# An mLSTM layer and a top-1 mixture of experts in one kernel: at most two of GpSimd's indirect DMAs under way, and a planner that knows more waits

## The chip, the cores and the metric

The kernel runs on one core of a Trainium2 chip. The metric is the device time of one execution in microseconds. The core's engines work side by side, each through its own instructions in order: TensorE (PE in the profile), VectorE (DVE), ScalarE (ACT), GpSimd (POOL), and SyncE (SP), which here only issues DMAs and reads two registers. A step on one engine that needs another's result waits for a semaphore.

## The reference

```python
# attention part: q, k, v, o_gate are (4, 8, 768, 40); i_gate, f_gate (4, 8, 768)
for t in range(S):
    m_new = np.maximum(f_gate[:, :, t] + m, i_gate[:, :, t])
    f_stab = np.exp(f_gate[:, :, t] + m - m_new)
    i_stab = np.exp(i_gate[:, :, t] - m_new)
    C = f_stab * C + i_stab * outer(v_t, k_t)        # one 40 x 40 state for each batch and head
    n = f_stab * n + i_stab * k_t
    denom = np.maximum(np.abs(n @ q_t), 1.0)
    y[:, :, t] = sigmoid(o_gate_t) * (C @ q_t) / denom
# the experts: x is y as 3072 rows of 320; 8 experts with 1024 hidden units
logits = x @ w_gate + modality_bias[modality_id]
e_idx = np.argmax(logits, axis=1)
gate_w = softmax(logits)[row, e_idx]
for e in range(8):
    h = np.maximum(x[e_idx == e] @ w1[e], 0.0)
    out[e_idx == e] = gate_w * (h @ w2[e])
```

## The kernel before

`still_arm` is the part that runs for inputs like these; a general part stands behind a branch and runs only if the first one finds that its assumptions don't hold (the word `bword`, computed by `checks`, `check_light`, `check_sums` and `verdict`).

*The work.* The 3072 tokens are cut in 24 chunks of 128. For each chunk, `light` (L1945) or, for the first 64 tokens of each batch, `special` (L2043, L2058) computes the rows of y. `token_rows` gates and divides two chunks at a time: DVE multiplies by the gate (L1961), POOL multiplies by the reciprocal denominators (L1976), and ACT and DVE split each row into a high and a low float16 part (`rows`, L1979, L1624, L1982). `scatter_rows` (L1997) then writes each chunk's rows by an indirect DMA of POOL to `x_s` in DRAM, sorted by modality, since the two modalities go nearly always to one expert each (classes A and B).

*The experts.* The sorted rows are taken in 15 tiles (`STREAM`): A and B in turn, four tiles of 128 rows first, then ten of 256, and a last one of 96. The tiles numbered 0 to 2 get their rows straight from SBUF by products with selection matrices (`select`, L2112, L2120, copied by ACT into `xt`, L2123, L2124). Later tiles get them by a transposing DMA from `x_s` (`load_tile`, L2096), with the token numbers (`load_ids`, L2102); these wait for the scatters of the chunks that the tile needs. `logits` (L2151 and DVE steps) computes each row's gate. `expert` runs the products with w1 into `H` (L2197), ACT's `hh` (L2202) and DVE's `hl` (L2204), which are the high and the low part of the hidden values, the products with w2 into `O` (L2214), ACT's scaling into `ob` (L2221, three buffers), and an indirect DMA of POOL to the output rows (L2222). All products with weights run three times or so, on high and low halves; `load_w` loads the weights of A and then of B in eight pieces each (L1902, through seven `stage` buffers) and splits them (ACT L1903, DVE L1904). Before that SP reads each expert's number from `e_i` (L1858).

*The odd row.* `odd_row` computes the one row that may have gone to a third expert. When all tiles have their gates, DVE sums what marks it (`fpr`, `fs5`), PE spreads it over partitions (L2246), POOL gathers the row into `xrow` by an indirect DMA (L2256), SP loads that expert's whole w1 and w2 (L2264, L2266), DVE does the products (L2269 to L2277), PE sums over partitions (L2280), ACT scales (L2282), and POOL scatters (L2283).

*The order.* Every step is added to a `Plan` with its engine, a duration from a formula, and the names it reads and writes. `Plan.run` computes how late each step may start (`late`, counted back from the end), subtracts `early`, and then simulates: on each engine, in order of time, the ready step with the smallest `late + bias` goes next. `bias` includes `NUDGE`, a number for single steps by their index. `lk=True` says that a step of DVE or POOL can't run beside such a step of the other; the simulation then holds it back. `lat` is added to a step's end. The instructions are emitted in the simulated order, and each engine runs them in that order. `SOON` (20.0) is the `early` of the chunks from 14 on and of most of the odd row; `HOLD` (200) keeps a step from being started earlier than its `late` plus 200. `idle_products` puts products on zeros where the plan sees PE idle between 4 and 60 us (L1731).

Of the kernel before, what the change touches and what calls it, by code (L numbers as in the profile page):

```python
# [16 lines left out]
ALU = mybir.AluOpType  # L17
# [20 lines left out]
class Plan:  # L38
# [6 lines left out]
    DMA_KB = 380.0  # L45
    AHEAD = 200.0
# [33 lines left out]
    def run(self):  # L80
# [29 lines left out]
        dma_free = 0.0  # L110
        port = {"DVE": 0.0, "POOL": 0.0}
        order, start, end = [], [0.0] * n, [0.0] * n
        while len(order) < n:
            best = None
            for name, e in engines.items():
                if not e["wait"] and not e["ready"]:
                    continue
                s = e["free"]
                if not e["ready"]:
                    s = max(s, e["wait"][0][0])  # L120
                if best is None or s < best[0]:
                    best = s, name
            s, name = best
            e = engines[name]
            while e["wait"] and e["wait"][0][0] <= s + 1e-9:
                i = heapq.heappop(e["wait"])[1]
                heapq.heappush(e["ready"], (late[i] + ts[i]["bias"], i))
            i = heapq.heappop(e["ready"])[1]
            t = ts[i]
            if t["lk"]:  # L130
                s = max(s, port["POOL" if name == "DVE" else "DVE"] - self.HOP)
            start[i] = s
            fin = s + t["dur"]
            if t["lk"]:
                port[name] = fin
            e["free"] = fin
            if t["kb"] is not None:
                dma_free = max(dma_free, fin) + t["kb"] / self.DMA_KB
                fin = dma_free + self.DMA_FIRST
            fin += t["lat"]  # L140
            end[i] = fin
            order.append(i)
            for j in succ[i]:
                hop = 0.0 if ts[j]["eng"] == t["eng"] and t["kb"] is None else self.HOP
                ready_at[j] = max(ready_at[j], fin + hop)
# [1404 lines left out]
SOON = 20.0  # L1550
HINT = 12.0
RING = 12
# [41 lines left out]
def still_arm(tc, a, out):  # L1594
# [113 lines left out]
    def load_kv(pr):  # L1708
        dma(373, lambda: sy.dma_start(kvs[pr], a["kvs"][pr]), w=[f"kv{pr}"], bias=FIRST.get("k", 0) if pr == 0 else 0)
# [4 lines left out]
    def load_o(i):  # L1714
        dma(328, lambda: sy.dma_start(og[i % 4], a["ogl"][:, 2 * i:2 * i + 2]), w=[f"og{i % 4}"], bias=FIRST.get(f"o{i}", 0))
# [8 lines left out]
    plan.add("ACT", 1.4, lambda: s_.preload_act_table_set("exp_and_others"), (), ["table"], bias=-90)  # L1724
# [132 lines left out]
    dve(2, lambda: v.tensor_scalar(ss[:, 0:4:3], n1.broadcast_to([P, 2]), float(CAP), None, ALU.is_ge), r=["cum"], w=["ss"])  # L1857
    dve(2, lambda: v.scalar_tensor_tensor(e_i, kd, ss[:, 0:1], km4[:, 2:4], ALU.mult, ALU.add), r=["kd", "km4", "ss"], w=["e_i"])  # L1858
    dve(1, lambda: v.tensor_scalar(ssc, n1, float(CAP), float(CAP), ALU.is_ge, ALU.mult), r=["cum"], w=["ssc"])
# [4 lines left out]
    dve(2, lambda: v.tensor_scalar(ss[:, 1:3], n1.broadcast_to([P, 2]), float(CAP), None, ALU.is_lt), r=["cum"], w=["ss"])  # L1864
# [85 lines left out]
    def token_rows(i):  # L1950
# [37 lines left out]
        for c in (2 * i, 2 * i + 1):  # L1988
            scatter_rows(c)
        dve(640, lambda: v.tensor_reduce(sums[:, 2 * i:2 * i + 2], rows[:, cs, 0:DM], axis=AX.X, op=ALU.add, apply_absolute_value=True),  # L1990
            r=[f"rowh{c0}", f"rowh{c0 + 1}"], w=["sums"], bias=15, nb=45 if i < 4 else None)

    def scatter_rows(c):
        s = c % RING

        def scatter():
# [5 lines left out]
            disjoint("xs", ins)  # L2002
# [234 lines left out]
    def odd_row():  # L2237
# [3 lines left out]
        for i, (t, ks) in enumerate(((u25, ["cst"]), (kmall, [f"km{k}" for k in range(n_)]), (facs, [f"fac{k}" for k in range(n_)]),  # L2241
                                     (ids, [f"ids{k}" for k in range(n_)]))):
            dve(25, lambda i=i, t=t: v.tensor_tensor(fpr[:, 1 + i], fm, t, ALU.mult), r=fms + ks, w=["fpr"])
# [14 lines left out]
            bounds_check=2 * CAP + P - 1, oob_is_err=False), NC), r=["fp_i"] + [f"xs{c}" for c in range(NC)], w=["xrow"])  # L2258
# [9 lines left out]
        plan.early = 0.0  # L2268
# [7 lines left out]
        for f in range(1, NFC):  # L2276
            dve(320, lambda f=f: v.scalar_tensor_tensor(facc, fw2[:, f], fh[:, f:f + 1], facc, ALU.mult, ALU.add), r=["og0", "fh"], w=["facc"], lk=True)  # L2277
        plan.early = SOON
# [10 lines left out]
    def checks():  # L2289
        dve(24, lambda: v.tensor_tensor(okc, cum, lo_f, ALU.is_ge), r=["cum", "cst"], w=["okc"])  # L2290
        dve(24, lambda: v.tensor_tensor(ra, cum, hi_f, ALU.is_le), r=["cum", "cst"], w=["ra"])
# [101 lines left out]
    for k in range(ntile):  # L2393
        while issued < ntile and issued <= k + PRE:
# [16 lines left out]
    def emit(some):  # L2411
        with tc.manual_schedule():
            for i in some:
# [3 lines left out]
                plan.tasks[i]["fn"]()  # L2417

    cut = sum(plan.start[i] < HINT for i in order)
# [147 lines left out]
```

## Time and profile before

| | |
|---|---|
| median of 3 runs | 223.29 us (223.13, 223.29, 226.51) |
| the profiled execution | 222.62 us |
| its span, first to last instruction | 220.9 us |
| PE, DVE, ACT, POOL busy | 206.7, 142.1, 97.0, 86.1 us |
| mean granted TensorE clock | 0.992 |
| DMA | 31.50 MB, mean 143 GB/s |
| POOL's indirect DMAs | 24 of rows, 25 of outputs, 2 of the odd row |

The profile is of one execution. A row of a timeline has the start and the length in us, the engine, the line, the operation, out<-in, and in brackets the idle time of the engine before it and what ended it. "q" behind an engine's name is its queue of instructions that do no arithmetic. In the chain of work that ended last, each piece is what the next one waited for, or the instruction before it on the same engine; "issue" is time in which nothing was waited for that the profile shows.

### The profile page before, as it was taken

The page shows a single profiled execution, that of the slowest core. Times are in us where ns is not written, and L with a number is a line of the kernel's source. Part 1 is how long each engine was busy: PE and PEld are TensorE (multiplying, and loading weights), DVE is VectorE, ACT ScalarE, POOL GpSimd, SP SyncE. Part 2 cuts the span into 40 slices and gives each one's busy share as a digit, 9 for nine tenths or more (in the row PEclk, how much of TensorE's full clock was granted, in tenths as well). Part 3 has the DMA queues.
Part 4 walks back from the last instruction along what each step waited for, and adds up shares of the span by engine and source line. Part 5 has one row for each costly group of instructions (what it writes and reads, how often), then busy time and mean ns, then how long its engine had stood idle before and what let it go on. Part 6 is the DMA issues. An engine that isn't in the chain of part 4 may idle for free.

```text
span 220.9 us, 5482 instructions
## 1 busy us (share of the span) xinstructions
PE 206.7 (94%) x2139; PEld 167.2 (76%) x2139; DVE 142.1 (64%) x421; ACT 97.0 (44%) x200; POOL 86.1 (39%) x98
## 2 busy tenths in 40 slices
PE   7987699999999999999999999999999999998960
PEld 2875589888887877878878768878878787785840
DVE  4789799998679463566386438425324858629960
ACT  2567688684255553342754313314553223143210
POOL 6458569421106716345048723526030120410321
PEclk9999999999999999999999999999999999999996
DMA  6989997989400659202774493202840010493100
GB/s 181 362 273 362 382 381 132 324 144 265 129 0 34 169 164 222 100 3 91 157 133 132 127 224 79 60 34 91 124 87 32 0 59 3 128 309 132 61 0 13
DMA packets 29783, 31.50 MB, mean 143 GB/s; under 512 B 21862, under 2 KB 22408, under 8 KB 29496
## 3 DMA queue, kind: packets, MB, share of 16 engines
q1 hardware_dynamic: 27176, 22.89, 38.9%
q0 software_dynamic: 2432, 8.13, 10.3%
q8 instruction: 18, 0.29, 0.6%
q14 instruction: 13, 0.11, 0.2%
q10 hardware_dynamic: 144, 0.07, 0.1%
HBM read 19.17 MB, written 8.43 MB: 125 GB/s over the span
## 4 chain that ended last, share of the span: by engine, by line
PE 68%; issue 14%; DMA 5%; POOL 2%; SPq 2%; DVE 2%; ACT 2%; another core or an unknown queue 1%; POOLq 1%; DVEq 0%
PE H L2197 32%; PE O L2214 28%; PE Y L1945 3%; DMA stage<-in_w1p 3%; DMA og<-in_ogl 3%; POOL out L2222 2%; PE M L2151 2%; SPq L1902 1%; PE Y L2043 1%; PE Y L2058 1%; POOLq L2407 1%; DVE hl L2204 1%; PE Y L1810 1%; PE O L2120 0%
## 5 line engine op out<-in xcount | busy, mean ns | idle before, releaser
L2204 DVE SCALAR_TENSOR_TENSOR hl<-H,hh 128x512 f16<-128x512 f32 (+1 forms) x50 | 33.9, 682 | 30.2 <-ACT hh L2202 25.6
L2214 PEld LDWEIGHTS <-hh 128*128 128x128 f16 (+1 forms) x400 | 38.6, 99 | 13.9 <-issue 0.5
L2202 ACT ACTIVATE hh<-H 128x512 f16<-128x512 f32 (+1 forms) x50 | 29.4, 592 | 42.1 <-PE H L2197 37.7
L2222 POOL DMA_INDIRECT out<-ob,ois x25 | 26.1, 1042 | 52.4 <-ACT ob L2221 35.9
L2197 PE MATMUL H<-xt,w1hB 128*128 128x256 f16 (+2 forms) x320 | 45.8, 251 | 0.1
L2197 PE MATMUL H<-xt,w1hA 128*128 128x256 f16 (+1 forms) x280 | 43.5, 257 | 0.3 <-issue 0.3
L2197 PE MATMUL H<-xt,w1lB 128*128 128x256 f16 (+2 forms) x192 | 40.6, 251 | 0.0
L2197 PE MATMUL H<-xt,w1lA 128*128 128x256 f16 (+1 forms) x168 | 37.9, 257 | 1.5 <-DVE w1lA L1904 1.5
L1976 POOL TENSOR_TENSOR xr<-xr,ab 128x640 f32<-128x640 f32 x12 | 17.1, 1424 | 38.9 <-DVE ab L1974 17.3
L2197 PEld LDWEIGHTS <-w1hB 128*128 128x128 f16 x320 | 28.5, 98 | 2.8
L1997 POOL DMA_INDIRECT x_s<-rows,pos_i x24 | 25.3, 1052 | 12.9 <-issue 7.0
L2214 PE MATMUL O<-w2hB,hh 128*128 128x320 f16 (+1 forms) x104 | 28.8, 299 | 0.0
L2214 PE MATMUL O<-w2lB,hh 128*128 128x320 f16 (+1 forms) x104 | 28.7, 299 | 0.0
L2197 PEld LDWEIGHTS <-w1hA 128*128 128x128 f16 x280 | 25.3, 98 | 3.3 <-issue 0.8
L2214 PE MATMUL O<-w2hA,hh 128*128 128x320 f16 x96 | 26.5, 299 | 0.0
L2214 PE MATMUL O<-w2lA,hh 128*128 128x320 f16 x96 | 26.5, 299 | 0.0
L2221 ACT ACTIVATE ob<-O,facs 128x320 f32<-128x320 f32 (+1 forms) x25 | 13.1, 526 | 30.6 <-PE O L2214 20.1
L2214 PEld LDWEIGHTS <-hl 128*128 128x128 f16 (+1 forms) x200 | 19.2, 99 | 8.7 <-DVE hl L2204 1.8
L2197 PEld LDWEIGHTS <-w1lB 128*128 128x128 f16 x192 | 18.7, 98 | 1.6 <-issue 0.3
L2197 PEld LDWEIGHTS <-w1lA 128*128 128x128 f16 x168 | 16.4, 98 | 3.1 <-DVE w1lA L1904 1.7
L2214 PE MATMUL O<-w2hB,hl 128*128 128x320 f16 (+1 forms) x104 | 17.1, 299 | 0.7 <-DVE hl L2204 0.7
L2214 PE MATMUL O<-w2hA,hl 128*128 128x320 f16 x96 | 15.3, 299 | 0.2 <-DVE hl L2204 0.2
(198 smaller groups left out, 294.0 us busy)
## 6 DMA issues: line engine op xcount, KB each, us to landing
qg<-in_ql SPq DMA_DIRECT2D x11, 384.0 KB
og<-in_ogl SPq DMA_DIRECT2D x12, 320.0 KB
stage<-in_w1p SPq DMA_DIRECT2D x8, 384.0 KB
stage<-in_w SPq DMA_DIRECT2D x8, 320.0 KB
stage<-in_w1t SPq DMA_DIRECT2D x1, 1280.0 KB
og<-in_w SPq DMA_DIRECT2D x1, 1280.0 KB
kvs<-in_kvs SPq DMA_DIRECT2D x2, 364.5 KB
sp<-in_spq SPq DMA_DIRECT2D x4, 160.0 KB
```

Of the source, the lines that this page charges most:

```text
L1810: t_.matmul(u3[0:120, g], lhsT=kw[pr][rs, 3 * g:3 * g + 3].rearrange("p h d -> p (h d)"), rhs=kvs[pr][rs, 9 * D + HQ * g:9 * D + HQ * (g + ...
L1902: dma(n // 2, lambda sv=sv, src=src: sy.dma_start(sv, src()), r=[f"reg{c}"], w=[f"stage{k}"])
L1945: t_.matmul(y[p0:p1, HQ * g:HQ * g + w], lhsT=q[0:k, j, g, p0:p1], rhs=s[0:k, g, 0:w], start=(g == 0 and e == 0), stop=(g == 2 and e == n ...
L1976: lane((320 if lane is dve else 290) * n, lambda z=z, f=f, n=n: f(x4[:, z].rearrange("p c h d -> p (c h) d"), x4[:, z].rearrange("p c h d ...
L1997: ins = g_.indirect_dma_start(out=x_s[:, :], out_offset=bass.IndirectOffsetOnAxis(ap=pos_i[:, c:c + 1].bitcast(U32), axis=0), in_=rows[:, ...
L2151: t_.matmul(M0[:, 16 * h:16 * h + 16], lhsT=x[:, b], rhs=wgr[:, b % 3].rearrange("p a e -> p (a e)"), start=(h == 0 and b == 0), stop=(h = ...
L2197: t_.matmul(hp3[:, i], lhsT=l, rhs=r, start=(i == 0 and q == 0), stop=(i == g - 1 and q == 7), skip_group_check=True)
L2202: act(g * n, lambda fl=fl, hp3=hp3: s_.activation(hh[:, fl, 0:n], hp3, AF.Relu), r=[nb], w=[f"hh{j}{f}" for f in range(f0, f0 + g)])
L2204: dve(g * n, lambda fl=fl, hp3=hp3: v.scalar_tensor_tensor(hl[:, fl, 0:n], hp3, 0.0, hh[:, fl, 0:n], ALU.max, ALU.subtract), r=[nb] + [f"h ...
L2214: t_.matmul(op[0:z, 0:DM], lhsT=t[:, f, P * h:P * h + z], rhs=w[:, f], start=(i == 0), stop=(i == 23))
L2221: act(400, lambda h=h, op=op, o=o: s_.mul(obs[o][0:z], op[0:z, 0:DM], facs[0:z, s["q0"] + h:s["q0"] + h + 1]), r=[no, f"fac{k}"], w=[f"ob{ ...
L2222: swdma(164, lambda h=h, o=o: disjoint("outf", g_.indirect_dma_start(out=out[:, :], out_offset=bass.IndirectOffsetOnAxis(ap=ois[0:z, s["q0 ...
```

## The change

1. **At most two under way.** When the instructions are emitted, each indirect DMA of POOL gets a dependency on the one two before it: it is issued when that one has landed. The planner does the same in its simulation (`OUT`, `sent`).
2. **What the planner knows.** DVE's steps with immediates or two operands from SBUF get `lk=True` (`ss`, `e_i`, `ssc`, parts of `odd_row` and `checks`); a step of POOL that may not run beside one of DVE starts 0.17 us behind its end (`LEAD`), not 0.13 ahead of it; four steps get a latency `lat` (the first `kvs`, the first two `og`, the gather of the odd row, its last sum).
3. **The odd row sooner.** Its steps get `early` 30 (`ODD`), where most had 20 and the products 0. `SOON` is 30 for 20.
4. **No explicit table load.** ACT's `preload_act_table_set` (L1724) goes; all later steps' indices fall by one.
5. **Priorities anew.** `NUDGE` has other numbers for many steps. `sums` of the later chunks may not start before 110 us in the plan.

```diff
 NUDGE = {
-    5: -33, 34: 162, 35: 57, 36: 44, 38: 34, 43: -8, 45: -116, 52: -7, ...
+    5: -33, 33: 453, 34: 199, 35: 44, 37: 34, 42: -8, 44: -116, 51: 21, ...
...
+    LEAD = 0.17
+    OUT = 2
...
             if t["lk"]:
-                s = max(s, port["POOL" if name == "DVE" else "DVE"] - self.HOP)
+                s = max(s, port["POOL"] - self.HOP if name == "DVE" else port["DVE"] + self.LEAD)
+            far = name == "POOL" and t["kb"] is not None
+            if far and len(sent) >= self.OUT:
+                s = max(s, sent[-self.OUT])
...
                 fin = dma_free + self.DMA_FIRST
+                if far:
+                    sent.append(fin)
...
-SOON = 20.0
+SOON = 30.0
+ODD = 30.0
...
-    plan.add("ACT", 1.4, lambda: s_.preload_act_table_set("exp_and_others"), (), ["table"], bias=-90)
...
-    dve(2, lambda: v.tensor_scalar(ss[:, 1:3], n1.broadcast_to([P, 2]), float(CAP), None, ALU.is_lt), r=["cum"], w=["ss"])
+    dve(2, lambda: v.tensor_scalar(ss[:, 1:3], n1.broadcast_to([P, 2]), float(CAP), None, ALU.is_lt), r=["cum"], w=["ss"], lk=True)
...
-            r=[f"rowh{c0}", f"rowh{c0 + 1}"], w=["sums"], bias=15, nb=45 if i < 4 else None)
+            r=[f"rowh{c0}", f"rowh{c0 + 1}"], w=["sums"], bias=15, nb=45 if i < 4 else 110)
...
-            bounds_check=2 * CAP + P - 1, oob_is_err=False), NC), r=["fp_i"] + [f"xs{c}" for c in range(NC)], w=["xrow"])
+            bounds_check=2 * CAP + P - 1, oob_is_err=False), NC), r=["fp_i"] + [f"xs{c}" for c in range(NC)], w=["xrow"], lat=3.0)
...
-        plan.early = 0.0
...
-        plan.early = SOON
...
             if issued == ntile:
                 check_sums()
+                plan.early = ODD
                 odd_row()
                 plan.early = SOON
...
-                plan.tasks[i]["fn"]()
-
+                ins = plan.tasks[i]["fn"]()
+                if plan.tasks[i]["eng"] == "POOL" and plan.tasks[i]["kb"] is not None:
+                    if len(sent) >= plan.OUT:
+                        tc.add_manual_dep(ins.ins, sent[-plan.OUT].ins.name,
+                                          mybir.DependencyInfo(mybir.DependencyClass.Sync, mybir.DependencyReason.DATA),
+                                          reason="GpSimd's DMAs under way")
+                    sent.append(ins)
+
+    sent = []
```

More of the change, by code (lines that the diff above doesn't have):

```diff
@@ L1702, in disjoint @@
         tc.add_to_no_dep_group(group, ins.ins)
+        return ins
     dma(64, lambda: s_.dma_start(gq, a["gsq"]), w=["gq"], eng="ACT", bias=-99)
@@ L1708, in load_kv @@
     def load_kv(pr):
-        dma(373, lambda: sy.dma_start(kvs[pr], a["kvs"][pr]), w=[f"kv{pr}"], bias=FIRST.get("k", 0) if pr == 0 else 0)
+        dma(373, lambda: sy.dma_start(kvs[pr], a["kvs"][pr]), w=[f"kv{pr}"], lat=0.5 if pr == 0 else 0.0, bias=FIRST.get("k", 0) if pr == 0 else 0)
     def load_q(i):
@@ L1714, in load_o @@
     def load_o(i):
-        dma(328, lambda: sy.dma_start(og[i % 4], a["ogl"][:, 2 * i:2 * i + 2]), w=[f"og{i % 4}"], bias=FIRST.get(f"o{i}", 0))
+        dma(328, lambda: sy.dma_start(og[i % 4], a["ogl"][:, 2 * i:2 * i + 2]), w=[f"og{i % 4}"], lat=0.9 if i < 2 else 0.0, bias=FIRST.get(f"o{i}", 0))
     load_kv(0)
@@ L1856, in still_arm @@
     ss, ssc = small([4], "ss"), small([1], "ssc")
-    dve(2, lambda: v.tensor_scalar(ss[:, 0:4:3], n1.broadcast_to([P, 2]), float(CAP), None, ALU.is_ge), r=["cum"], w=["ss"])
-    dve(2, lambda: v.scalar_tensor_tensor(e_i, kd, ss[:, 0:1], km4[:, 2:4], ALU.mult, ALU.add), r=["kd", "km4", "ss"], w=["e_i"])
-    dve(1, lambda: v.tensor_scalar(ssc, n1, float(CAP), float(CAP), ALU.is_ge, ALU.mult), r=["cum"], w=["ssc"])
+    dve(2, lambda: v.tensor_scalar(ss[:, 0:4:3], n1.broadcast_to([P, 2]), float(CAP), None, ALU.is_ge), r=["cum"], w=["ss"], lk=True)
+    dve(2, lambda: v.scalar_tensor_tensor(e_i, kd, ss[:, 0:1], km4[:, 2:4], ALU.mult, ALU.add), r=["kd", "km4", "ss"], w=["e_i"], lk=True)
+    dve(1, lambda: v.tensor_scalar(ssc, n1, float(CAP), float(CAP), ALU.is_ge, ALU.mult), r=["cum"], w=["ssc"], lk=True)
     dve(24, lambda: v.scalar_tensor_tensor(ra, C0[:, 32:32 + NC], ssc, cumx[:, 0:NC], ALU.add, ALU.add), r=["cum", "cum0", "H2", "ssc"], w=["ra"])
@@ L2001, in scatter @@
             tc.declare_no_dep(ins.ins, group="reads", reason="rows of tiles that need this chunk are loaded later, others are not in it")
-            disjoint("xs", ins)
+            return disjoint("xs", ins)
         swdma(168, scatter, r=[f"rowh{s}", f"rowl{s}", f"id{s}", "rowz", "pos_i"] + (["prefill0", "prefill1"] if c > 10 else []), w=[f"xs{c}"])
@@ L2079, in behind @@
                               reason="the chunk's rows")
+        return ins
     def no_late(ins, need):
@@ L2242, in odd_row @@
                                      (ids, [f"ids{k}" for k in range(n_)]))):
[L2243 removed]
+            dve(25, lambda i=i, t=t: v.tensor_tensor(fpr[:, 1 + i], fm, t, ALU.mult), r=fms + ks, w=["fpr"], lk=True)
         dve(125, lambda: v.tensor_reduce(fs5, fpr, axis=AX.X, op=ALU.add), r=["fpr"], w=["fs5"])
@@ L2276, in odd_row @@
         for f in range(1, NFC):
-            dve(320, lambda f=f: v.scalar_tensor_tensor(facc, fw2[:, f], fh[:, f:f + 1], facc, ALU.mult, ALU.add), r=["og0", "fh"], w=["facc"], lk=True)
-        plan.early = SOON
+            dve(320, lambda f=f: v.scalar_tensor_tensor(facc, fw2[:, f], fh[:, f:f + 1], facc, ALU.mult, ALU.add), r=["og0", "fh"], w=["facc"], lk=True, lat=2.5 if f == NFC - 1 else 0.0)
         n2, y2 = take("Y")
@@ L2289, in checks @@
     def checks():
-        dve(24, lambda: v.tensor_tensor(okc, cum, lo_f, ALU.is_ge), r=["cum", "cst"], w=["okc"])
-        dve(24, lambda: v.tensor_tensor(ra, cum, hi_f, ALU.is_le), r=["cum", "cst"], w=["ra"])
+        dve(24, lambda: v.tensor_tensor(okc, cum, lo_f, ALU.is_ge), r=["cum", "cst"], w=["okc"], lk=True)
+        dve(24, lambda: v.tensor_tensor(ra, cum, hi_f, ALU.is_le), r=["cum", "cst"], w=["ra"], lk=True)
         dve(24, lambda: v.tensor_tensor(okc, okc, ra, ALU.mult), r=["ra"], w=["okc"], lk=True)
@@ L2416, in emit @@
                     zeros(to, w, to is not M0)
-                plan.tasks[i]["fn"]()
+                ins = plan.tasks[i]["fn"]()
[5 more added lines that the diff above has]
+                    sent.append(ins)
+    sent = []
     cut = sum(plan.start[i] < HINT for i in order)
```

28 rows, old and new, of the table NUDGE are left out of this document.

## The prediction

> **What bounds the kernel now.** I read the page's busy shares first, then busy time by stage, then who TensorE (PE) waited for, then the chain and the timelines of the stages where PE was idle.
>
> ```profile
> span 220.9 us, 5482 instructions
> PE 206.7 (94%) x2139; PEld 167.2 (76%) x2139; DVE 142.1 (64%) x421; ACT 97.0 (44%) x200; POOL 86.1 (39%) x98
> PEclk9999999999999999999999999999999999999996
> ```
>
> PE is busy 94% of the span at the full granted clock, and no other engine reaches 65%. So only PE's 14.2 us without work, and what it does without need, can be won. The stages (columns: stretch, length, busy us and instructions of PE, its weight loads, DVE, ACT, POOL; clock, DMA share, GB/s):
>
> ```profile
> 4.00:16.00 12.00, 11.01 (x106) 8.67 (x105) 8.85 (x37) 6.87 (x20) 6.13 (x12) 1.00 0.93 306
> 16.00:27.40 11.40, 8.05 (x95) 6.45 (x92) 10.02 (x21) 7.77 (x16) 7.94 (x7) 1.00 1.03 373
> 27.40:54.50 27.10, 27.10 (x360) 23.44 (x360) 25.50 (x60) 19.48 (x36) 12.72 (x12) 1.00 0.88 246
> 54.50:120.00 65.50, 65.43 (x650) 53.65 (x648) 41.78 (x115) 30.84 (x68) 27.96 (x25) 1.00 0.45 114
> 120.00:130.00 10.00, 9.47 (x85) 7.20 (x84) 4.10 (x16) 3.05 (x6) 5.83 (x6) 1.00 0.60 158
> 130.00:180.00 50.00, 50.00 (x545) 40.68 (x544) 24.24 (x70) 17.43 (x37) 15.85 (x16) 1.00 0.30 70
> 180.00:200.00 20.00, 19.98 (x177) 16.52 (x174) 12.47 (x47) 7.24 (x13) 3.06 (x3) 1.00 0.47 155
> 200.00:214.30 14.30, 12.91 (x134) 9.52 (x132) 13.00 (x45) 2.53 (x6) 2.96 (x3) 1.00 0.10 39
> 214.30:220.90 6.60, 0.00 (x0) 0.00 (x0) 0.16 (x1) 0.52 (x1) 0.94 (x1) 0.73 0.05 11
> ```
>
> Between 27.4 and 214.3 us PE is idle for 0 + 0.07 + 0.53 + 0 + 0.02 + 1.39 = 2.01 us. The 184.9 us of products there are untouched by the change. What is left to win is those 2.0 us and the start: from 16.0 to 27.4 PE idles 3.35 us, with the DMA engines full (1.03 of their time, 373 GB/s). The last 6.6 us hold the last scatter and the landing of its rows; nothing in the diff shortens them. The waits by name (us in all, times, longest):
>
> ```profile
> PE O L2120 <- ACT xt L2123: 1.8, 1, 1.8
> PE H L2197 <- DVE w1lA L1904: 1.5, 1, 1.5
> PE O L2214 <- DVE hl L2204: 0.9, 2, 0.7
> PE Y L2280 <- DVE facc L2277: 0.7, 1, 0.7
> ```
>
> The first two are the start, the next two the end (the odd row and the DVE steps round it).
>
> **The change, part by part.**
>
> *Steps with immediates marked `lk`.* The 1.5 us wait has its cause in the timelines of DVE and POOL:
>
> ```profile
> 17.57 1.67 DVE L1864 TENSOR_SCALAR ss<-cumx 128x2 f32<-128x2 f32 x1
> 17.93 1.28 POOL L1976 TENSOR_TENSOR xr<-xr,ab 128x640 f32<-128x640 f32 x1
> 19.80 0.95 DVE L1904 SCALAR_TENSOR_TENSOR w1lA<-stage,w1hA 128x768 f16<-128x768 f32 x1
> 20.80 0.23 PE L2197 MATMUL H<-xt,w1lA 128*128 128x128 f16 x1 [1.53 <-DVE w1lA L1904]
> ```
>
> A step on two numbers took 1.67 us, because it overlapped POOL's 1.28 us multiplication: it ended 0.03 us after it. The low weights (L1904) behind it, and PE's first products, came that much later. The planner did not know this kind of step waits; now it does, and can put L1864 elsewhere. That removes the 1.53 us wait, but only a part is gained: the last pieces of the first expert's weights come with full DMA queues anyway, as the chain of this stage shows:
>
> ```profile
> 15.45 5.91 DMA stage<-in_w1p
> 21.38 0.84 ACT w1hA L1903
> 22.23 2.16 another core or an unknown queue
> 24.57 0.60 ACT xt L2123
> 25.22 1.01 PE O L2120 x15
> ```
>
> A piece of weights issued at 15.45 lands 5.91 us later. ACT then stands 2.16 us for something the profile can't name, and PE's 1.8 us wait is its consequence. The new order doesn't remove a cause that I can name here. For the start as a whole, nothing and all of its named waits (1.53 + 1.82 = 3.35 us) are the bounds; I take **-1.5 us**, the first wait, since its cause is the one the planner now sees.
>
> *At most two indirect DMAs under way.* The trace of before has no such wait, so its cost is bounded from the rows of POOL and of SP's queue:
>
> ```profile
> 16.66 1.24 POOL L1997 DMA_INDIRECT x_s<-rows,pos_i  x1 [1.74 <-ACT w2hA L1903]
> 19.37 1.01 POOL L1997 DMA_INDIRECT x_s<-rows,pos_i  x1 [0.16 <-issue]
> 25.04 0.97 POOL L1997 DMA_INDIRECT x_s<-rows,pos_i  x1 [0.30 <-issue]
> 37.65 1.00 POOL L1997 DMA_INDIRECT x_s<-rows,pos_i  x1 [0.17 <-issue]
> 40.23 1.44 POOL L1997 DMA_INDIRECT x_s<-rows,pos_i  x1 [0.30 <-issue]
> 31.04 1.33 SPq L2096 DMA_TRANSPOSE xt<-x_s  x1
> 44.53 2.80 SPq L2096 DMA_TRANSPOSE xt<-x_s  x2
> 54.53 1.75 PE H L2197 x16
> ```
>
> The transposes wait for the scatters (1.0 and 1.8 us of SP's queue in these two places), so the last scatter before each landed no later than its start: 25.04 to 31.04 is 6.0 us, 40.23 to 44.53 is 4.3 us. Six scatters stand from 16.66 to 25.04. With two under way, the third waits for the first, and so on: at 4.3 us each they issue at 16.66, 19.37, 20.96, 23.67, 25.26, 27.97, the last 2.9 us later; at 6.0 us each, at 22.66, 25.37, 28.66, 31.37, the last 6.3 us later. In the next batch of four, the one at 40.23 waits for that of 37.65 to land (41.95): 1.7 us. Behind the waiting scatters stand POOL's multiplications of rows, then those rows' own scatters, then SP's transposes, then the fifth tile's products at 54.53. If that order stays, the transposes come 4.6 to 8.0 us later. They have 10.0 us, of which 1.4 go to the first of the two transposes and 4.3 (an estimate, the scatters' own landing) to its flight: 4.3 us of slack, 2.8 if PE is there 1.5 us earlier. So the price is 0 to 5.2 us. I take **0**: the planner now counts these waits when it picks its order, so it can run multiplications ahead of a blocked scatter. Less than nothing would need the loads to be faster for it; no row shows that. Later batches, of two to five scatters, lie in stages with the DMA engines at 0.30 to 0.60 of their time, where PE has tiles ready; I cost them at 0, and if that cover is gone they cost what the fifth tile's do. The waits themselves sit on POOL, which is 39% busy.
>
> *The odd row sooner.* The tail end of PE, by the timeline:
>
> ```profile
> 190.14 1.05 POOL L2256 DMA_INDIRECT xrow<-x_s,fp_i  x1 [10.24 <-issue]
> 198.24 0.23 DVE L2269 TENSOR_TENSOR xf<-xrow 128x64 f32<-128x64 f16 x1 [2.85 <-DMA xrow<-x_s,fp_i]
> 203.05 0.45 PE L2214 MATMUL O<-w2hB,hl 128*128 128x320 f16 x2 [0.66 <-DVE hl L2204]
> 211.81 0.70 PE L2280 MATMUL Y<-facc,ones_f 128*2 128x320 f32 x2 [0.70 <-DVE facc L2277]
> 215.16 0.94 POOL L2222 DMA_INDIRECT out<-ob,ois  x1 [0.99 <-ACT ob L2221]
> ```
>
> DVE stood 2.85 us for the gathered row, which landed 8.1 us after its issue; that pushed `hl` and cost PE 0.66 us, and the row's sum came 0.70 us after PE wanted it. Due 10 us earlier (30 for 20; in its middle 30 for 0), with 3.0 us of latency told to the planner, both waits should go: **-1.36 us**, bounds -1.39 (all of this stage) and 0. Its 0.70 us of product stays on PE, which is late next. The last scatter waits for `ob` alone. The limit adds a wait for the scatter two before it, which is of the tile before, a tile's products earlier; with the DMA engines at 0.10 of their time in this stage I cost that at 0. If the odd row's gather and the rows of two tiles met the loads of its weights again (8.1 us to land), the third buffer of `ob` is the cover.
>
> *No explicit table load.* It was not at the start:
>
> ```profile
> 198.18 1.28 ACT L1724 ACT_TABLE_LOAD   x1
> 199.47 0.60 ACT L2202 ACTIVATE hh<-H 128x512 f16<-128x512 f32 x1
> ```
>
> The planner put this load, which nothing waits for, where ACT was free, and it held up one `hh` by at most its own 1.28 us. That `hh` feeds the `hl` whose 0.66 us wait is counted above, so nothing more is won: 0. If the load was the whole cause of that wait, it goes all the same.
>
> *Priorities anew, latencies, nudges.* About 1100 steps in another order. In the middle PE idles 0.60 us; I take **-0.2**, bounds -0.6 and +0.6 (as much again).
>
> **Sum** against the profiled execution (222.62 us: the 220.9 of span and 1.7 round it): -1.5 + 0 - 1.36 - 0.2 = -3.06, so 219.6. The three runs shown have a median of 223.29, 0.67 above that execution; taken off the median, **220.3 us**. The range of this case alone is 218.8 to 222.
>
> **Rivals.**
>
> *All of the start goes.* The wait ACT can't explain stands in the midst of the six scatters, so fewer under way may end it. Then 3.35 + 1.36 + 0.6 = 5.3 us go: 218.0. For it: PE's two waits there are all that holds it back. Against it: the DMA engines are full in that stage. The Trainium skill, "DMA: Bandwidth & Descriptors", section "SWDGE vs HWDGE vs iDMA", says that POOL's descriptors and the others' feed different queues of each DMA engine, which takes them in turn; by that, two scatters hold the same share of the engines as six, and the loads would not be faster. No row here tells it apart; it lowers this chance.
>
> *One set of waits for another.* The new order meets steps that the planner still mis-sizes, as L1864 was: only the end's gain, offset by the middle's +0.6 and by a start that is held by its loads. 223.29 - 1.36 + 0.6 = 222.5, to 223.5.
>
> *Slower: the limit takes the fifth tile's rows.* POOL keeps its order, the scatters land in 6.0 us, and the transposes of 44.53 start after 52. PE then stands up to 5.2 us at its 54.53: 220.3 + 5.2 = 225.5. It decides from transposes later than 47.3 (2.8 us of slack), and the whole is slower than before from a stall of 3.0 us. For it: the burst of six is real and POOL works in order. Against: the planner counts the limit. The Trainium skill, "TensorE: Matmul & The Clock Gate", Part 1, says a window of 3.4 us without work halves the clock; by it such a stall would cost some 1.7 us more. Here the clock is 1.00 in every stage and the longest wait 1.8 us, so no run shows it.
>
> *The limit does nothing.* If scatters land faster than two issues apart, no wait is ever met; the time is then the forecast's.
>
> **Chances.** Forecast 0.52, all of the start 0.2, one set for another 0.16, slower 0.12. The range reaches from 217.3 to 225.5: it leaves out the lower part of the second case and the worst of the fourth. Two per cent is about what a measurement of this kernel can tell from no change: 218.8 and 227.8. Faster: 0.2 and 0.05 of the forecast's lower edge; slower: 0.05, the fourth case with a longer stall; within: 0.7.
>
> **What would show it.** L1864 short and outside POOL's multiplications, and PE's first products without the 1.5 us; POOL's scatters in pairs, with idle time ended by a DMA, and transposes before 47; ACT's nameless 2.16 us gone or not; DVE not waiting for `xrow`, no wait of PE for `hl` or `facc` after 200; one table load. Wrong would be: a new wait of PE between 45 and 60 us, or a start that ends no earlier than 25 us.

## The result, and the profile after

The changed kernel takes 221.86 us (median of 18 runs, 219.60 to 222.82), the kernel before 224.30 us in the same comparison (222.59 to 227.56): a ratio of 0.9892, with a 95% interval of 0.9866 to 0.9918. The forecast was 220.3 us and "within 2%", and both hold. The ratio that the forecast implies, 220.3 to 223.29, is 0.9866, at the edge of the interval. The kernel before ran at medians from 221.7 to 224.3 us in the comparisons below, so ratios are compared, not times.

The profiled execution took 221.87 us, 0.75 less than the one of before, where the medians differ by 2.44: the profiled execution of before lies at the low end of its 18 runs. Lines of the changed kernel stand 12 to 14 lower in the code: H is L2211, `hh` L2216, `hl` L2218, O L2228, the scatter of rows L2010, that of outputs L2236, POOL's multiplication L1989, the low weights L1917. The page and the waits of PE:

```profile
span 220.2 us, 5491 instructions
PE 207.4 (94%) x2142; PEld 167.7 (76%) x2142; DVE 140.1 (64%) x421; ACT 96.4 (44%) x199; POOL 86.5 (39%) x98
```

```profile
PE H L2211 <- DVE w1lA L1917: 1.1, 1, 1.1
PE H L2211 <- issue: 0.9, 2, 0.6
PE Y L2071 <- DVE aw L1637: 0.6, 1, 0.6
PE M L2374 <- DVE Bs L1637: 0.4, 1, 0.4
```

The four waits that were named before are gone or shorter: `xt` (1.8), `hl` and `facc` are not there, `w1lA` has 1.1 for 1.5. Three new ones stand in their place, none of them at the start or the end. By stages (the columns are those shown for before; PE's idle time is the length less the first busy time):

```profile
16.00:27.40 11.40, 10.31 (x136) 8.82 (x134) 11.01 (x23) 8.66 (x20) 8.31 (x7) 1.00 1.00 354
27.40:54.50 27.10, 26.57 (x328) 21.78 (x325) 24.02 (x55) 19.05 (x35) 14.22 (x13) 1.00 0.91 268
54.50:120.00 65.50, 64.05 (x628) 51.94 (x626) 41.95 (x118) 30.29 (x67) 25.50 (x23) 1.00 0.41 111
120.00:130.00 10.00, 10.00 (x107) 8.34 (x106) 6.46 (x24) 3.40 (x7) 5.30 (x5) 1.00 0.15 49
130.00:180.00 50.00, 49.40 (x534) 40.01 (x533) 27.98 (x106) 17.66 (x39) 17.36 (x18) 1.00 0.39 84
200.00:213.60 13.60, 13.47 (x142) 10.45 (x139) 1.87 (x4) 3.11 (x7) 2.86 (x3) 1.00 0.07 24
```

PE's idle time is 1.09 us at the start (3.35 before) and 0.13 at the end (1.39), but 0.53 + 1.45 + 0 + 0.60 = 2.58 between (0.62 before; 180 to 200 us has 0.00 and 0.02). So 3.5 us of idle time were won and 2.0 given back in this execution; PE's busy time is 0.7 us longer (207.4 for 206.7), so the span is 0.7 us shorter and not 1.5. DVE has 1.87 us of work left after 200, where it had 13.00: the odd row is over by then.

The rows that the forecast named, from the timelines (one of ACT, two of DVE, two of POOL):

```profile
1.25 1.28 ACT L1800 ACT_TABLE_LOAD   x1 [1.25 <-PEq L2564]
```

```profile
16.74 0.16 DVE L1877 TENSOR_SCALAR ss<-cumx 128x2 f32<-128x2 f32 x1
186.60 0.23 DVE L2282 TENSOR_TENSOR xf<-xrow 128x64 f32<-128x64 f16 x1 [0.26 <-DMA xrow<-x_s,fp_i]
```

```profile
74.45 0.97 POOL L2010 DMA_INDIRECT x_s<-rows,pos_i  x1 [0.30 <-issue]
92.41 0.97 POOL L2236 DMA_INDIRECT out<-ob,ois  x1 [1.04 <-DMA x_s<-rows,pos_i]
```

`ss` is short, as foreseen, DVE waits 0.26 us for the gathered row instead of 2.85, and the table is loaded once, at 1.25 us. But the limit is half there: the scatter at 74.45 is the fourth in 4 us and waits for none, while an output scatter waits for a scatter of rows. All through the trace only pairs of different kinds wait. Scatters to one tensor are put in a group without dependencies among them (`disjoint`), and the added dependency seems to be dropped there too; that this is the reason was not tried by itself.

### The profile page after: what moved, and what is told of

Same layout as the page of the kernel before. It is cut to its first block, busy times and chain, and to the rows that moved or that the text cites. A ratio compares the mean times of both kernels' runs of the same rounds, so it can differ in the third digit from the quotient of the medians.

```text
span 220.2 us, 5491 instructions
## 1 busy us (share of the span) xinstructions
PE 207.4 (94%) x2142; PEld 167.7 (76%) x2142; DVE 140.1 (64%) x421; ACT 96.4 (44%) x199; POOL 86.5 (39%) x98
## 4 chain that ended last, share of the span: by engine, by line
PE 68%; issue 9%; DVE 8%; DMA 5%; POOL 4%; SPq 2%; ACT 0%; POOLq 0%; DVEq 0%
PE H L2211 31%; PE O L2228 26%; DMA x_s<-rows,pos_i 4%; PE Y L1958 3%; PE O L1744 2%; DMA ids<-x_s 2%; PE Y L2056 1%; SPq L2110 1%; DVE w2lA L1917 1%; POOL out L2236 1%; PE M L2165 1%; DVE rows L1637 1%; POOL xr L1989 1%; PE Y L2071 1%; DVE xr L1974 1%
## 5 line engine op out<-in xcount | busy, mean ns | idle before, releaser
L2218 DVE SCALAR_TENSOR_TENSOR hl<-H,hh 128x512 f16<-128x512 f32 (+1 forms) x50 | 33.7, 679 | 41.7 <-ACT hh L2216 36.8
L2236 POOL DMA_INDIRECT out<-ob,ois x25 | 25.7, 1029 | 63.4 <-ACT ob L2235 41.6
L2228 PEld LDWEIGHTS <-hh 128*128 128x128 f16 (+1 forms) x400 | 38.7, 99 | 15.5 <-issue 1.0
L2216 ACT ACTIVATE hh<-H 128x512 f16<-128x512 f32 (+1 forms) x50 | 29.5, 592 | 45.9 <-PE H L2211 39.7
L2211 PE MATMUL H<-xt,w1hB 128*128 128x256 f16 (+2 forms) x320 | 46.1, 251 | 0.0
L2211 PE MATMUL H<-xt,w1hA 128*128 128x256 f16 (+1 forms) x280 | 43.5, 257 | 0.9 <-issue 0.9
L2211 PE MATMUL H<-xt,w1lB 128*128 128x256 f16 (+2 forms) x192 | 40.7, 251 | 0.0
L2211 PE MATMUL H<-xt,w1lA 128*128 128x256 f16 (+1 forms) x168 | 38.0, 257 | 1.2 <-DVE w1lA L1917 1.1
L2010 POOL DMA_INDIRECT x_s<-rows,pos_i x24 | 26.7, 1112 | 14.4 <-issue 4.0
L2211 PEld LDWEIGHTS <-w1hB 128*128 128x128 f16 x320 | 28.2, 98 | 2.7
L1989 POOL TENSOR_TENSOR xr<-xr,ab 128x640 f32<-128x640 f32 x12 | 15.8, 1313 | 36.9 <-DVE fm L1637 15.9
L2228 PE MATMUL O<-w2hB,hh 128*128 128x320 f16 (+1 forms) x104 | 28.7, 299 | 0.3 <-ACT hh L2216 0.3
L2211 PEld LDWEIGHTS <-w1hA 128*128 128x128 f16 x280 | 25.6, 98 | 4.5 <-issue 1.7
L2228 PE MATMUL O<-w2lB,hh 128*128 128x320 f16 (+1 forms) x104 | 28.7, 299 | 0.0
L2228 PE MATMUL O<-w2lA,hh 128*128 128x320 f16 x96 | 26.5, 299 | 0.2 <-DVE w2lA L1917 0.2
L2228 PE MATMUL O<-w2hA,hh 128*128 128x320 f16 x96 | 26.5, 299 | 0.0
L2228 PEld LDWEIGHTS <-hl 128*128 128x128 f16 (+1 forms) x200 | 19.7, 99 | 7.6 <-DVE hl L2218 0.3
L2211 PEld LDWEIGHTS <-w1lB 128*128 128x128 f16 x192 | 18.7, 98 | 1.4
L2211 PEld LDWEIGHTS <-w1lA 128*128 128x128 f16 x168 | 16.4, 98 | 2.6 <-DVE w1lA L1917 1.3
L2228 PE MATMUL O<-w2hB,hl 128*128 128x320 f16 (+1 forms) x104 | 16.2, 299 | 0.0
L2228 PE MATMUL O<-w2hA,hl 128*128 128x320 f16 x96 | 15.1, 299 | 0.0
```

What stands on the lines that cost most here:

```text
L1989: lane((320 if lane is dve else 290) * n, lambda z=z, f=f, n=n: f(x4[:, z].rearrange("p c h d -> p (c h) d"), x4[:, z].rearrange("p c h d ...
L2010: ins = g_.indirect_dma_start(out=x_s[:, :], out_offset=bass.IndirectOffsetOnAxis(ap=pos_i[:, c:c + 1].bitcast(U32), axis=0), in_=rows[:, ...
L2211: t_.matmul(hp3[:, i], lhsT=l, rhs=r, start=(i == 0 and q == 0), stop=(i == g - 1 and q == 7), skip_group_check=True)
L2216: act(g * n, lambda fl=fl, hp3=hp3: s_.activation(hh[:, fl, 0:n], hp3, AF.Relu), r=[nb], w=[f"hh{j}{f}" for f in range(f0, f0 + g)])
L2218: dve(g * n, lambda fl=fl, hp3=hp3: v.scalar_tensor_tensor(hl[:, fl, 0:n], hp3, 0.0, hh[:, fl, 0:n], ALU.max, ALU.subtract), r=[nb] + [f"h ...
L2228: t_.matmul(op[0:z, 0:DM], lhsT=t[:, f, P * h:P * h + z], rhs=w[:, f], start=(i == 0), stop=(i == 23))
```

## The experiments

### The changed kernel again

> The changed kernel once more, unchanged, beside before. Open after the variant without the added waits: its profile lost 1.3 us by its first tile's second products (its third low part of the first weight matrix came 1.1 us later, at 25.35 instead of 24.25 us), and the first added wait of the changed kernel stands at 36 us, so this part of the loss can hardly be the waits'. Theory 'chance of arrivals': the start's loads land in another order from run to run; the changed kernel's own times then spread over 1.3 us or more, its profile here may show the same stall of about 1.4 us for w1lA, and its ratio to before lies at 0.990 to 0.999. Theory 'the waits': the ratio is that of the first comparison, 0.987 to 0.992, and the tile's milestones lie within 0.4 us of the first profile.

Measured: ratio 0.994 (0.9905 to 0.9975), 220.33 against 221.69 us. The interval overlaps that of the first comparison, 0.9866 to 0.9918: the gain is some 0.6 to 1.1 per cent. PE's waits, and the rows of DVE and POOL behind them:

```profile
PE H L2211 <- DVE w1lA L1917: 2.3, 2, 1.3
```

```profile
26.48 1.30 POOL L1989 TENSOR_TENSOR xr<-xr,ab 128x640 f32<-128x640 f32 x1
26.88 1.72 DVE L1917 SCALAR_TENSOR_TENSOR w1lA<-stage,w1hA 128x768 f16<-128x768 f32 x1 [1.09 <-ACT w1hA L1916]
```

and the same two steps in the first profile of the changed kernel:

```profile
25.61 0.96 DVE L1917 SCALAR_TENSOR_TENSOR w1lA<-stage,w1hA 128x768 f16<-128x768 f32 x1
26.33 1.36 POOL L1989 TENSOR_TENSOR xr<-xr,ab 128x640 f32<-128x640 f32 x1
```

The stall is back, with the same instructions in the same order. In the first profile DVE's step is through 0.24 us after POOL's begins; in the second, weights that came later let it begin beside POOL's, and it ends 0.82 us after POOL's end: as with `ss` in the profile of before, whose 1.67 us also lasted until POOL was done. In four of the five profiles with this start (this one, the one without added waits, the one with the odd row as before, the late limit below) PE waits 1.2 to 1.4 us more there. The start of the first profile was the lucky one.

The ends of tiles say what that is worth. Before, the first tile's second products end at 33.78 us and the fourth tile's at 54.53. In the first profile they end at 32.44 and 53.99, in the other four at 33.6 to 33.9 and 54.6 to 54.9. So in four profiles of five nothing is won up to the fourth tile. Behind it, up to PE's last product, the kernel before takes 159.7 us and the kernel run again 157.5: its whole gain lies there.

The Trainium skill, "SBUF — State Buffer", section "Who interferes with whom", says that a VectorE instruction with two inputs from SBUF contends with a GpSimd instruction that reads SBUF; both steps here are of these kinds, and their lengths (0.96 alone, 1.72 beside) agree.

### The added waits, left out and put in alone

```diff
-                    if len(sent) >= plan.OUT:
+                    if False:
```

> The changed kernel in its own order, with the added waits of POOL's indirect DMAs left out (the planner still counts them). Order theory (the gain of 1.1% is the new order at the start and the odd row at the end): no change from the changed kernel, ratio to before 0.985 to 0.995. Limit theory (fewer scatters under way shorten delays elsewhere): the gain goes, ratio 0.995 to 1.005. In the changed kernel's trace only a few of POOL's waits are ended by one of its DMAs (1.0 us at 92.4, 2.3 at 132.6, 1.1 at 154.8), so by the order theory at most these move, off PE's path.

Measured: ratio 1.0034 (1.0011 to 1.0057): the whole gain is gone, and not by a stray execution, since the nine runs lie between 223.50 and 223.93 us. PE's new waits, and two stretches of the middle:

```profile
PE H L2211 <- DVE w1lA L1917: 2.5, 2, 1.4
PE H L2211 <- issue: 2.1, 4, 0.7
```

```profile
60.00:100.00 40.00, 37.45 (x369) 30.11 (x367) 24.10 (x66) 19.03 (x43) 18.46 (x16) 1.00 0.43 111
```

The start is that of the kernel run again. From 60 to 100 us PE is idle for 2.55 us. In the changed kernel's two profiles this stretch has:

```profile
60.00:100.00 40.00, 38.96 (x383) 31.33 (x381) 25.32 (x64) 20.59 (x46) 18.37 (x16) 1.00 0.45 112
```

```profile
60.00:100.00 40.00, 40.00 (x404) 32.69 (x402) 25.95 (x67) 20.95 (x46) 18.85 (x16) 1.00 0.48 112
```

that is 1.04 and 0.00. Most of the loss has "issue" as its releaser: gaps of 0.4 to 0.7 us inside a tile's first products, at 77 and from 93 to 96 us, while POOL issues five or six indirect DMAs one behind the other, or right after. What PE waits for there the profile doesn't show. One candidate can be seen: a 16 KB transfer of the instruction queue comes at 97.7 us in the first profile of the changed kernel and at 98.6 here, when PE is at its 992nd and 982nd product; in three profiles without such gaps (run again, odd row as before, late limit) it comes at 94.0 to 94.8 us, at the 972nd or 973rd. Whether PE stood for its instructions, no run tests.

The same waits in the kernel before, the lines of the change in `emit` and nothing else:

> The kernel before with only the added waits, its own plan and order. Order theory: 0.998 to 1.003 of before. Limit theory: 0.988 to 0.995. A third outcome, slower by up to 1%, would say that the waits cost where the plan does not count them.

Measured: ratio 1.0009 (0.9982 to 1.0037), nothing that can be told from no change. By themselves the waits show no worth; in the new order they do.

### A limit that holds for all

```diff
+                far = plan.tasks[i]["eng"] == "POOL" and plan.tasks[i]["kb"] is not None
+                if far and len(sent) >= plan.OUT:
+                    mark = g_.memset(limit, 0.0)
+                    tc.add_manual_dep(mark.ins, sent[-plan.OUT].ins.name, ...)
                 ins = plan.tasks[i]["fn"]()
```

> The changed kernel, but with a limit that holds for every pair: ahead of each indirect DMA POOL clears one number and waits for the DMA two before it, of whatever kind (in the changed kernel's profile only pairs of different kinds wait). It adds 48 such clearings of some 0.1 us on POOL. Theory 'the limit is what helps' (few transfers side by side leave the loads their share): 0.983 to 0.990, and the first low weight parts come no later. Theory 'the order helps, waits only cost' : the third scatter, issued at 20.7 us, must wait until the first has landed at 23.1, each further one until some 5 to 7 us after the one two before it was issued; by the sixth POOL is 3 to 6 us behind, its products of xr and rows stand behind these waits, the first tile's rows come that much later, and the time is 1.005 to 1.03.

Measured: ratio 1.0133 (1.0088 to 1.0178), slower. Three rows of one chain, and two stretches (POOL, ACT, PE; the number behind POOL's count is the clock):

```profile
31.00 0.10 POOL L2432 MEMSET limit<- 128x1 f32 x1 [4.89 <-DMA x_s<-rows,pos_i]
```

```profile
34.05 0.72 ACT L1992 CAST rows<-xr 128x640 f16<-128x640 f32 x1 [5.34 <-POOL limit L2432]
```

```profile
39.51 0.45 PE L2228 MATMUL O<-w2hA,hh 128*128 128x320 f16 x1 [4.52 <-ACT hh L2216]
```

```profile
39.50:43.50 4.00, 3.99 (x16) 2.21 (x17) 4.00 (x5) 3.29 (x6) 3.59 (x7) 0.50 0.91 219
54.50:120.00 65.50, 65.50 (x661) 53.77 (x658) 43.43 (x123) 32.13 (x68) 25.02 (x39) 1.00 0.49 129
```

POOL waits 4.89 us for a scatter to land; its multiplication stands behind that, ACT's cast behind the multiplication, ACT's `hh` behind the cast, and PE behind `hh`. Then the clock is at half. This is the slower rival of the forecast, by another path (ACT's queue, at the second tile) and with nearly its price: the last product ends at 216.4 us, and at 211.4 with the late limit below. From 54.5 to 120 us PE has no gap at all. The start, though, is the best of all the runs: the first tile's second products end at 31.4 us. POOL's multiplication stands back there until 32.74, and DVE's low part of the weights, at 25.48, takes 0.96 us. Whether the loads were faster too, the run doesn't separate.

So the limit was tried from the ninth transfer on, issued at 36 us or later, behind the wait that held up ACT:

```diff
-                if far and len(sent) >= plan.OUT:
+                if far and len(sent) >= 8:
```

> The changed kernel with a limit that holds for every pair, but only from the ninth indirect DMA on (issued at 36 us or later); the first eight go as in the changed kernel. The kernel with the limit for all lost 7.3 us between its first and second tile, where ACT waited 5.3 us behind POOL, and then ran tiles 3 to 5 in 33.24 and tile 6 in 14.39 us, against 33.72 and 15.95 in the changed kernel's profile and 34.32 and 16.75 without added waits. Theory 'fewer transfers under way keep the middle free': tiles 3 to 5 in 33.2 to 33.4 and tile 6 in 14.4 us, PE without a wait of kind issue from 60 to 120 us, ratio 0.984 to 0.992. Rival 'the middle's stalls come by chance': tile 6 anywhere between 14.4 and 16.8 us, ratio 0.989 to 1.003. Rival 'POOL's waits cost something later': new PE waits behind rows or ois after 60 us, above 1.0.

```profile
60.00:100.00 40.00, 40.00 (x395) 32.58 (x393) 26.61 (x65) 21.05 (x46) 18.84 (x28) 1.00 0.37 102
```

```profile
80.73 0.10 POOL L2432 MEMSET limit<- 128x1 f32 x1 [3.01 <-DMA x_s<-rows,pos_i]
```

Measured: ratio 0.9929 (0.9896 to 0.9962). POOL waits up to 3 us, and nobody minds; PE is never idle between 36 and 180 us. Against the changed kernel (0.9892 and 0.994) no difference can be told. That fewer transfers under way keep the middle free agrees with the profiles: waits of kind "issue" of 2.1 us in sum without the added waits, 0.9 us and none in the changed kernel's two, none with the odd row as before, none with the whole limit. But the kernel with the same waits has 0.9 us in one profile and none in another, so chance has a part.

### The odd row

In the changed kernel, planned as in before:

```diff
-                plan.early = ODD
+                plan.early = 20.0
...
-            ..., w=["xrow"], lat=3.0)
+            ..., w=["xrow"])
...
+        plan.early = 0.0
...
-            ..., w=["facc"], lk=True, lat=2.5 if f == NFC - 1 else 0.0)
+            ..., w=["facc"], lk=True)
+        plan.early = 20.0
```

> The changed kernel with the odd row planned as in before (due 20 us early, no lag added, the last sum as in before), all else of the change in place. Theory as predicted: the end alone carries 1.4 to 1.5 us, PE's waits for hl and facc at 203 and 212 us come back, tiles 0 to 10 stay within 0.3 us of the changed kernel, ratio to before 0.993 to 0.999. Rival 'something else ends last': the end stays as fast, ratio 0.987 to 0.992.

```profile
PE O L2228 <- DVE hl L2218: 0.6, 1, 0.6
PE Y L2294 <- DVE facc L2291: 0.5, 1, 0.5
```

Measured: ratio 1.0041 (1.001 to 1.0072), against 0.994 for the changed kernel beside it: the odd row is worth 0.010. In times it is less: the medians are 222.04 and 220.33 us, 1.7 apart, and the spans of the two profiles 220.2 and 218.9, 1.3 apart. Both waits are back, at 188.9 and 198.4 us. With the odd row as before, the rest of the change wins nothing (1.0041), just as the rest wins nothing without the added waits (1.0034): the gain needs both. What the new order costs without either, no run measures.

The reverse, the earlier odd row alone in the kernel before:

```diff
+                plan.early = 30.0
                 odd_row()
...
-            ..., w=["xrow"])
+            ..., w=["xrow"], lat=3.0)
...
-        plan.early = 0.0
...
-        plan.early = SOON
```

> The kernel before with the odd row's steps due 30 us earlier in all its parts and 3.0 us of latency told for its gather; the rest of the plan as before. Order theory: the waits of PE after 200 us go (0.66 for hl, 0.70 for facc), -1.4 us, ratio about 0.994. Limit theory has nothing to say of it beyond less than half of the gain. If the odd row's work only moves the wait to other products: 1.000.

```profile
205.09 1.23 PE L2278 MATMUL Y<-facc,ones_f 128*2 128x320 f32 x2 [3.99 <-DVE facc L2276]
```

```profile
205.00:207.50 2.50, 2.41 (x7) 0.82 (x8) 2.50 (x6) 0.43 (x1) 0.41 (x1) 0.50 0.00 0
```

Measured: ratio 1.0215 (1.0174 to 1.0256). The planner put PE's product of the odd row ahead of a tile's last products, DVE's sum came 4 us after its place, and half clock followed. An earlier due time moves the step that waits too, and here it made the stall it was to remove. This kernel lacks the 2.5 us of latency that the change tells for the last sum, and the new priorities; which of them it misses was not tried.

### No table load

```diff
-    plan.add("ACT", 1.4, lambda: s_.preload_act_table_set("exp_and_others"), (), ["table"], bias=-90)
+    plan.add("ACT", 1.4, lambda: None, (), ["table"], bias=-90)
```

> The kernel before without the instruction of the explicit table load, its plan unchanged. Both theories: 0.997 to 1.001, since the load at 198 us holds one hh by at most 1.28 us and that shows at most in PE's 0.66 us wait for hl at 203. A rival says that the load is the cause of that whole wait: -0.66 us, ratio 0.997, and the wait for hl at 203 gone from the trace.

```profile
203.13 0.45 PE L2214 MATMUL O<-w2hB,hl 128*128 128x320 f16 x2 [0.66 <-DVE hl L2204]
```

Measured in the kernel before: ratio 1.0027 (0.9994 to 1.006). No change clear of noise, and the wait for `hl` stays at 0.66 us to the digit: the load was not its cause.

### The priorities, and the start

Before's priorities in the changed kernel:

```diff
-    5: -33, 33: 453, 34: 199, 35: 44, 37: 34, ...
+    5: -33, 33: 162, 34: 57, 35: 44, 37: 34, ...
```

> The changed kernel with before's hand-set priorities (their numbers moved to the same steps), so all else of the change under the old priorities: on SP the loads of tile 2's qg and og stand again behind seven pieces of weights, as in before. Theory 'the priorities carry the start': the stall of 1.8 us for xt and with it the start's 1.3 us come back, ratio 0.995 to 1.004. Theory 'the planner's knowledge carries the start' (the immediate steps known): the start keeps it, 0.987 to 0.993. Old priorities that fit no longer could also unsettle the middle: then above 1.005, with PE's new waits after 55 us.

Measured: ratio 1.1688 (1.1638 to 1.1737). PE waits 7.2 us for one word of the checks and 5.6 for a tile's gates; the numbers fit one plan only, and the run says nothing on the start. The start's priorities alone, in the kernel before:

```diff
-    5: -33, 34: 162, 35: 57, 36: 44, 38: 34, ...
+    5: -33, 34: 453, 35: 199, 36: 44, 38: 34, ...   # the change's up to step 100, then before's
```

> The kernel before with the change's priorities for the first hundred steps only: on SP the loads of tile 2's qg and og go ahead of the weights as in the changed kernel; the scatters stay in before's order, and planner, odd row and waits are before's. Theory as predicted (the order of the loads is worth 1.3 us): the wait of 1.8 us for xt goes, the first tile's second products end at 32.2 to 32.7 instead of 33.78 us, and if nothing later moves the ratio is 0.992 to 0.996. Rival 'one set of waits for another': the weights, two loads further back, arrive too late; PE waits twice for w1lA, over 2 us in sum, the first tile ends at 33.4 us or later, ratio 0.997 to 1.005. Priorities set for another plan could also unsettle what follows: above 1.005.

```profile
17.47 2.07 DVE L1851 TENSOR_SCALAR ss<-cumx 128x2 f32<-128x2 f32 x1
```

Measured: ratio 1.0076 (1.0048 to 1.0105). The loads stand in the new order and PE no longer waits 1.8 us for `xt`, but `ss` collides again (2.07 us), and the first tile's second products end at 36.6 instead of 33.8 us. PE's waits up to there are 1.3 us for `rows`, 0.9 for `hh` and 0.5 for `w1lA`, and the tile's first products begin at 23.05 us instead of 19.00. So the order of the loads by itself gains nothing; how much of the loss is `ss` and how much priorities made for another plan, the run doesn't separate.

Two attempts to mend the start, both on top of the late limit. First, the third and fourth scatter held back too:

```diff
-                if far and len(sent) >= 8:
+                if far and (len(sent) in (2, 3) or len(sent) >= 8):
```

> As the kernel before this one, and the limit on the third and fourth scatter too (held until the first and second have landed at about 23 to 24 us, some 2.5 us later than in the changed kernel); the fifth to eighth go freely. With the limit for all, the first tile's second products ended at 31.4 us, against 32.4 and 33.6 in two profiles of the changed kernel, since the low part of the first weights came in time. Theory 'scatters and weight loads share the queue's engines': the first tile ends at 31.0 to 32.0 us, tile 2 no later than 1 us behind, ratio 0.978 to 0.988. Rival 'what is held back is late in the next tile': rows of tile 2 wait, the first gain is given back by the fourth tile's end (54.0 to 54.6 us in the changed kernel), ratio 0.988 to 1.0.

```profile
PE O L2228 <- DVE w2lA L1917: 2.0, 1, 2.0
PE H L2211 <- DVE w1lA L1917: 1.4, 2, 1.1
```

Measured: ratio 1.0047 (1.0024 to 1.007). The waits for the first weights' low part are 1.4 us in sum, not 2.3, but a low part of the second weights costs 2.0 us, and the first tile ends at 36.1 us. Then POOL's fourth multiplication held until DVE's fourth low part is done:

```diff
+        if len(muls) == 4:
+            tc.add_manual_dep(ins.ins, lows["wA3"].ins.name, ...)
```

> The kernel with the limit from the ninth transfer on, and one wait more: POOL's fourth product of xr, which began at 26.3 to 26.8 us in the profiles, waits for VectorE's fourth low part of the first weights. In the profiles that part took 0.96 us where it began at 25.61, ahead of POOL's product, and 1.72, 1.79, 2.50 and 2.65 us where its weights came 0.3 to 0.6 us later and POOL's product of 1.28 us ran beside it; PE waited 1.2 to 1.4 us more for it, and the first tile ended at 33.6 to 33.9 instead of 32.44 us. Theory 'the two engines stand in each other's way, and the arrival of the weights decides': the part takes 0.95 us in every run, the first tile ends at 32.3 to 32.9 us, POOL's fourth scatter behind it goes up to 0.9 us later; ratio to before 0.984 to 0.990, that is 0.003 to 0.008 under the kernel without this wait. Rival 'the late weights alone are the stall': the part takes 0.95 us but begins as late as before, ends under 0.5 us sooner, and the ratio stays at 0.990 to 0.996. Rival 'POOL's lateness moves on': the first tile ends sooner, and the next one waits for its rows as long; 0.992 to 1.0.

Timeline of DVE, three steps, and the wait of PE (L1919 is here the low part, L2239 the product O):

```profile
27.62 0.96 DVE L1919 SCALAR_TENSOR_TENSOR w1lA<-stage,w1hA 128x768 f16<-128x768 f32 x1 [1.02 <-ACT w1hA L1918]
29.23 1.24 DVE L1988 TENSOR_SCALAR ab<-ab 128x16 f32<-128x16 f32 x1
31.70 1.51 DVE L2184 SCALAR_TENSOR_TENSOR lg<-lg,bias 128x16 f32<-128x16 f32 x1
```

```profile
34.00 0.30 PE L2239 MATMUL O<-w2lA,hh 128*128 128x320 f16 x1 [1.96 <-DVE w2lA L1919]
```

Measured: ratio 0.997 (0.993 to 1.001). The low part takes 0.96 us, as it should, but POOL's multiplication (28.66 to 30.43 us) and its low parts of rows (31.62 to 33.17), later now, meet two later steps of DVE: 1.24 and 1.51 us, where they took 0.21 and 0.17 in the changed kernel run again. PE waits 1.96 us for the last low part instead. The collision moved; neither attempt beats the changed kernel.

## Why the prediction was right or wrong

*The start, -1.5 us: wrong as a gain, and hidden by luck in the first profile.* The cause named, `ss`, is gone as foreseen, and the nameless wait of ACT with PE's 1.8 us behind it went too, which the forecast had not counted on. In the first profile PE's idle time from 16 to 27.4 us fell by 2.26 us, and the first tile ended 1.3 us sooner. But in four of five profiles a wait of 1.2 to 1.4 us more for `w1lA` took its place: the rival "one set of waits for another", with the mechanism of `ss` on the next step. There the first tile ends at most 0.2 us sooner than before, and the fourth no sooner. The step that failed is that the first wait, once removed, is won. The low parts behind it come no sooner: the first of the four begins at 19.80 us before and at 21.06 in the kernel run again, and the fourth is done at 27.84 and 28.60, since it meets POOL there.

*The limit, 0: wrong as a part of this order, right for the order of before.* The bounds had no gain in them, "less than nothing would need the loads to be faster for it". The runs show 1.0034 without the waits and 0.9892 and 0.994 with them. The gain doesn't come from the loads at the start, where the waits don't act, but from 60 to 100 us. The step "later batches at 0" failed: PE had tiles ready there and still stood. And "scatters in pairs" was wrong: the change does what it says between kinds only, half a case of the last rival. The upper bound of 5.2 us is near what a limit that holds cost (5.0 us), but by chance: the cost fell on ACT's queue, not on the transposes.

*The odd row, -1.36: right.* Both waits are gone, and PE's idle time of this stage fell by 1.26 us. Planned as before, the odd row costs 1.3 us by the profiles and 1.7 by the medians.

*The table load, 0: right. The priorities, -0.2 within 0.6: too narrow.* The middle lost 2.0 us in the first profile (0.62 to 2.58). From 60 to 200 us PE is never idle in the kernel run again, where it was idle for 0.62 before; so the same order lost 2.0 in one profile and won 0.6 in another.

*The sum, -3.06.* The first profiles differ by -0.75, the medians by -2.44 and -1.36. The forecast came out 1.6 us low and inside its range, but that it is so near is in part luck. Half of it, the start, isn't there in four profiles of five. The kernel run again gains 2.3 us behind the fourth tile, where the forecast had 1.56 (the odd row and the priorities).

Two slips in the working: it says that the clock is 1.00 in every stage, but its own last stage, with no products, has 0.73; and the 217.3 us at which it lets the range begin comes from no sum that it shows.

## What to carry to other kernels

Before a stall is counted as won, look at which step comes next on the same two engines: where DVE and POOL share a stretch, a shifted POOL step hits another small DVE step, and a 0.2 us step became a 1.5 us one here. Then look at a milestone further on, such as the end of the fourth tile: idle time that goes in one stage can come back in the next. One profile is one draw: two profiles of the same kernel differed by 1.2 us in the start and 1.0 us in the middle, as much as the parts to be judged. In this kernel a limit on transfers paid where nobody waited for their landing, and cost its whole length where the issuing engine also feeds the others in order.

## What the runs showed of the hardware

Waits of PE and the clock behind them can be set side by side. With the limit for all, a wait of 4.52 us stands with 0.50 of the clock from 37.99 to 44.82 us; with the earlier odd row alone, one of 3.99 us with 0.50 from 204.51 to 207.92. A wait of 2.03 us (third and fourth scatter held, 31.32 to 33.35) brought half clock as well, and one of 1.96 us (POOL's multiplication held, 32.04 to 34.00) did not. The stretches of half clock are 6.83, 3.41 and 3.41 us long, one or two times the same length. So here are two stretches of 3.41 us of each of the last two kernels, laid to end or begin where the clock changed in that trace (in the second, 54 lengths ahead of its change at 217.97 us):

```profile
30.33:33.74 3.41, 1.30 (x8) 0.58 (x6) 3.41 (x8) 3.04 (x5) 3.11 (x4) 1.00 0.89 349
33.74:37.15 3.41, 3.41 (x22) 2.46 (x20) 3.41 (x5) 1.47 (x2) 3.24 (x3) 0.50 0.58 161
```

```profile
30.23:33.64 3.41, 1.81 (x13) 1.07 (x11) 3.38 (x7) 3.41 (x6) 2.95 (x5) 1.00 0.80 296
33.64:37.06 3.42, 3.06 (x37) 2.41 (x37) 3.42 (x6) 2.08 (x3) 3.25 (x3) 1.00 0.59 166
```

In the first, PE is busy for 1.30 us of the stretch and half clock follows; in the second the wait falls across two stretches, with 1.81 and 3.06 us busy, and the clock stays. The Trainium skill, "TensorE: Matmul & The Clock Gate", Part 1, gives about 3.4 us without work as what halves the clock, in a window that runs freely. The length agrees with the 3.41 us here; but a stretch with 1.30 us of products in it was enough. That the share of such a stretch decides, and so where a wait happens to fall, is an estimate from these two traces; no run tests it.
